# Four heads per group, masked queries, and part of the exponentials on VectorE, in an attention block with a gated MLP on one core

## The chip, the cores and the metric

One core of a Trainium2 chip runs the whole program. The metric is the time of one execution on the device in microseconds (us), as a median over runs. The kernel before takes 1070.86 us (1070.6 to 1070.98, 3 runs). All executions quoted here are recorded as fast; none was recorded as slow. TensorE is PE in the profile, its weight loads PEld, VectorE is DVE, ScalarE is ACT, GpSimd is POOL, and SP is the engine whose queue issues the DMA transfers.

## The reference, cut to what matters

```python
def reference(A_x, A_wqkv, A_wo, B_x, B_w1, B_w2, B_w3, B_w4):
    # S = 2048 tokens, D = 640, H = 32 heads of 20, F = 1536
    xn = layernorm(A_x)
    q, k, v = heads(xn @ wqkv)                            # 32 x 2048 x 20
    p = softmax(q @ k.T * 20 ** -0.5)                     # 32 x 2048 x 2048
    s = merge(p @ v) @ wo
    h = gelu(layernorm(xn) @ w1)                          # tanh form
    x1 = xn + shifted(h) @ w2
    g = silu(x1 + gelu(layernorm(x1) @ w3) @ w4)
    return A_x + s * g
```

The attention has 32 x 2048 x 2048 = 134 million exponentials. A tile of 128 keys x 512 queries x two heads is one ScalarE instruction of 1,024 elements on each of 128 partitions, so there are 1,024 such tiles.

## The kernel before

Both kernels are task graphs. Python code declares tasks with an engine, a duration, the regions they read and write, and a due time. A list scheduler inside the program then fixes the order of each engine's queue before anything runs, and each queue executes strictly in order. The heart of the kernel before:

```python
# queries of each head, masked to the head's rows, on GpSimd
T("pool", c_pool(512), lambda e, ...: e.tensor_scalar(QTP[:, qb, i, :], QT[:, st, q0:q0 + 512],
                                     self.maskh[:, j:j + 1], 0.0, op0=ALU.mult, op1=ALU.add), ...)
for kt in range(NT):                          # 16 key tiles
    for a in range(2):                        # two pairs of heads
        for jj in range(2):
            def fn(e, ...):                   # scores: four column tiles, K = 128
                for c in range(4):
                    ins = e.matmul(pb[32 * c:32 * c + 32, 0:512], KT[:, st, kt * 128 + 32 * c: kt * 128 + 32 * c + 32],
                                   QTP[:, qb, i, :], start=True, stop=True, tile_position=(0, 32 * c))
        T("act", c_act(1024), lambda e, ...: e.activation(PT[:, slot, :], self.psum[:, 1024 * sb:1024 * sb + 1024], AF.Exp,
                                                          scale=cfg.scale), ...)
    # then the product with V of the four heads: four column tiles, M = 22
...
def gelu_chain(...):                          # gelu from ScalarE's tanh: x*x, *, * on VectorE, tanh, a last multiply
    T("act", c_act(512), lambda e: e.activation(thb, wb, AF.Tanh, scale=math.sqrt(2.0 / math.pi)), ...)
```

Of the kernel before, what the change touches and what calls it, by code (L numbers as in the profile page):

```python
# [12 lines left out]
class _Heap:  # L13
# [58 lines left out]
"""Static task-graph planner for raw-BASS kernels.  # L72

Usage:
    pl = Planner()
    buf = pl.sbuf("name", nbytes)            # arena allocation (with free())
    pl.task(engine, dur_ns, emit_fn, reads=[atoms], writes=[atoms], due=...)
    pl.finish(nc, ...)                        # schedule + emit inside nc.Block

Atoms are hashable keys naming disjoint memory regions.  Dependencies  # L80
(RAW / WAR / WAW) are derived from the canonical order in which tasks are
declared.  A list scheduler then picks a per-engine order; every engine
stream is emitted with semaphore waits derived from vector clocks.
"""
# [6 lines left out]
class Task:  # L91
# [3 lines left out]
                 "acq", "rel", "stream", "sidx", "cls", "nbytes")  # L95

    def __init__(self, tid, eng, dur, fn, reads, writes, due, name, lat, is_dma):
# [24 lines left out]
        self.nbytes = 0  # L122


class Planner:
    def __init__(self):
        self.tasks = []
        self.last_writer = {}
        self.readers = defaultdict(list)
        self.pe_psum_atoms = set()  # L130
        self.arena_size = None
        self.free_list = []
        self.bufs = {}
        self.ghost = []
        self.atom_owner = {}
        self.buf_atoms = defaultdict(set)
        self.buf_range = {}
        self.buf_inherit = {}
        self.pools = {}
        self.count_instr = False  # L140
        self.dma_bw = 280.0
        self.dma_lat0 = 1900.0
        self.strict_engines = ("pe",)
        self.cls_penalty = 1e9
        self.streams = {}

# [53 lines left out]
    def task(self, eng, dur, fn, reads=(), writes=(), due=None, name="", lat=0.0,  # L200
             is_dma=False, acq=None, rel=None, stream=None, after=(), cls=0, nbytes=0):
# [3 lines left out]
        t.nbytes = nbytes  # L205
        if is_dma and nbytes:
            t.lat = self.dma_lat0 + nbytes / self.dma_bw
        t.acq = acq
# [6 lines left out]
        if stream is not None:  # L215
# [3 lines left out]
            t.sidx = len(lst) + 1  # L219
# [43 lines left out]
    def schedule(self, verbose=False):  # L263
# [13 lines left out]
        for t in reversed(tasks):  # L277
# [8 lines left out]
            t.prio = d  # L286
        for t in tasks:
            if t.cls and t.eng in self.strict_engines:
                t.prio = t.prio + self.cls_penalty
# [11 lines left out]
        done = 0  # L301
        WINDOW = 48
        while done < n:
            best = None
            for e in ENGINES:
# [7 lines left out]
                k = 0  # L313
                while h and k < WINDOW:
# [5 lines left out]
                    if t.acq is not None:  # L320
                        ps = pstate[t.acq[0]]
                        ft = min(x[0] for x in ps)
                        if ft > rt:
                            rt = ft
                    if rt <= tf + 1e-9:
                        cand = (tf, item)
                        break
# [10 lines left out]
            if st == INF:  # L338
                _log("[plan] DEADLOCK: all candidates blocked on pools")
                for e2 in ENGINES:  # L340
                    for it in ready[e2][:5]:
                        t2 = tasks[it[1]]
                        _log("   ready", e2, t2.name, "acq", t2.acq is not None)
                unsched = [t2 for t2 in tasks if t2.start is None]
                _log("   unscheduled:", len(unsched), [t2.name for t2 in unsched[:10]])
                for t2 in tasks:
                    if t2.start is not None and t2.acq is not None and id(t2.acq[1]) in held:
                        rel = [t3 for t3 in tasks if t3.rel is t2.acq[1]]
                        _log("   held by tile of", t2.name, "release task", [ (r.name, r.start, [tasks[p].name for p in r.preds if tasks[p].start is None]) for r in rel])
# [5 lines left out]
            if t.acq is not None:  # L355
                pname, handle = t.acq
                ps = pstate[pname]
                si = min(range(len(ps)), key=lambda i: ps[i][0])
                ft, rel_tid = ps[si]
                handle.slot = si  # L360
                held[id(handle)] = (pname, si)
                ps[si] = (INF, None)
                if rel_tid is not None:
                    t.preds.add(rel_tid)
                    tasks[rel_tid].succs.append((t.id, True))
            t.start = st
            t.finish = st + t.dur
            if t.is_dma and t.nbytes:
# [7 lines left out]
            if t.rel is not None:  # L376
                pname, si = held.pop(id(t.rel))
# [20 lines left out]
    def plan_sync(self, sems, dma_sems):  # L398
# [28 lines left out]
        for tid in glob:  # L427
# [3 lines left out]
            for p in sorted(t.preds, key=lambda i: (-tasks[i].finish, -tasks[i].pos)):  # L431
# [6 lines left out]
                elif pt.is_dma:  # L438
                    key = ("dma", p)
                    need = 16  # L440
# [19 lines left out]
            elif t.is_dma:  # L460
                snap[("dma", tid)] = 16
# [6 lines left out]
    def emit(self, nc, block, sems):  # L468
# [20 lines left out]
        def run_engine(ename, eng):  # L489
            cnt = _Cnt(eng) if self.count_instr else None  # L490
            for tid in self.order[ename]:
# [9 lines left out]
                if t.is_dma:  # L501
                    if t.dma_sem is not None:
                        assert ins is not None, t.name
                        ins.then_inc(t.dma_sem, 16)
# [24 lines left out]

"""Kernel generator (development version).  Uses dev.planner.Planner."""  # L530

# [3 lines left out]
I32 = mybir.dt.int32  # L535
# [13 lines left out]
class Cfg:  # L549
    def __init__(self, S=2048, D=640, H=32, F=1536, dbg=()):  # L550
# [7 lines left out]
        self.HPS = 6  # L558
        self.RPH = 21
        self.NST = (H + self.HPS - 1) // self.HPS  # L560
        self.NQUAD = H // 4
        self.TG = min(4, self.NT)
        self.NG = self.NT // self.TG
        self.scale = self.DH ** -0.5
        self.OFFSET = 60.0
        self.dbg = set(dbg)
        self.T0 = 25000.0
        self.STEP = 1000.0
        self.NSTEP = self.NQC * self.NQUAD * self.NT * 2
        self.TEND = self.T0 + self.NSTEP * self.STEP  # L570
        self.B_START = 0.25
        self.B_END = 0.8


def c_dve(n, kind="psum"):
    if kind == "psum" or kind == "1x":
        return 65 + 1.042 * n
    if kind == "2x":
        return 65 + 0.521 * n
    if kind == "4x":  # L580
        return 65 + 0.2605 * n
    if kind == "recip":
        return 65 + 6.25 * n
# [3 lines left out]
def c_act(n):  # L587
    return 70 + 0.8333 * n


def c_pe(ninstr, N):
    return ninstr * max(29.0, 0.105 * N)
# [6 lines left out]
class Gen:  # L599
# [24 lines left out]
    def free(self, name):  # L624
        self.pl.free(name)
        self.views.pop(name, None)
# [24 lines left out]

    def build(self, plan_only=False):
        nc, cfg, pl = self.nc, self.cfg, self.pl
        with contextlib.ExitStack() as es:
            ARENA = 212000
            self.arena = es.enter_context(nc.sbuf_tensor("arena", [128, ARENA], U8))
            self.psum = es.enter_context(nc.psum_tensor("psum", [128, 4096], FP32))
            pl.init_arena(ARENA)
            self.W0 = 5
            pl.pool("W", 3)  # L660
            self.program()
# [7 lines left out]
            _log(f"[gen] tasks={len(pl.tasks)} waits={pl.n_waits} dma_sems={pl.n_dma_sems} est={ms/1e3:.1f}us")  # L669
            with nc.Block() as block:  # L670
                pl.emit(nc, block, sems)

    def program(self):
        cfg = self.cfg
        self.setup_consts()
        self.alloc_persistent()
        self.load_inputs()
        self.ln1_and_transpose()
        self.load_weights_attn()
        self.alloc_attn()  # L680
        self.v_proj()
        for st in range(cfg.NST):
            self.stack_prep(st, evac_eng="act" if st == 0 else "dve")
        for nm in self.ln1_defer:
            self.free(nm)
        self.free("xnT")
        self.free("Wv")
        self.free("xbar")
        self.free("xbar_bf")
        self.out_atoms = []  # L690
        self.cur_cls = 1
        self.b_branch()
        self.cur_cls = 0
        self.attention()
        self.debug_dump()

    def setup_consts(self):
        cfg = self.cfg
        T, A = self.T, self.A
        ident = self.alloc("ident", [128], BF16)  # L700
        ones = self.alloc("ones_bf", [128], BF16)
        self.ident = ident
# [4 lines left out]
        HPS, DH = cfg.HPS, cfg.DH  # L707
        AUG0 = HPS * DH
        onesf = self.alloc("ones_f", [8], FP32)
        T("pool", 200, lambda e: e.memset(onesf[:, :], 1.0), writes=[A("ones_f")], name="onesf")  # L710
        E6 = self.alloc("E6", [8], FP32)
# [865 lines left out]
```

## Time and profile before

| kernel before | value | where it is read |
|---|---|---|
| time | 1070.86 us | median of 3 runs |
| first exponential starts | 47.1 us | timeline of ScalarE |
| stage: first exponential to the end of the last | 1013.9 us | timeline of ScalarE |
| tail after the last exponential | 11.0 us | timeline of ScalarE |
| wait of the exponentials themselves | 17.7 us | costliest groups |
| busy: ScalarE, TensorE, VectorE | 96%, 87%, 51% | busy shares |

Start, stage and tail add up, but for rounding, to the span of the profiled execution, 1071.9 us. A stage is a count of exponentials multiplied by a price, plus what ScalarE does besides, plus what it waits. The prediction shows the profile lines for these figures.

### The profile page before, as it was taken

The numbers are of one execution on the slowest core, as the hardware profiler recorded it, in microseconds if no ns is written. First come the engines' busy times: TensorE is split into PE (matmuls) and PEld (weight loads), VectorE is DVE, ScalarE is ACT, GpSimd is POOL, SyncE is SP. The second block draws the span as 40 slices with busy tenths as digits, with TensorE's granted clock in tenths as the row PEclk, the third lists the DMA queues.
The fourth block names the chain that finished last, engine by engine and source line by source line (L and its number), as shares of the span: only waits on it lengthen the run. The fifth ranks groups of instructions, "written<-read, shape, count | busy, mean of one in ns | idle before, by whom it ended". The sixth has DMA issues, their size and how long they took to land.

```text
span 1071.9 us, 38329 instructions
## 1 busy us (share of the span) xinstructions
PE 937.1 (87%) x17672; PEld 395.9 (37%) x17672; DVE 547.6 (51%) x1272; ACT 1024.4 (96%) x1175; POOL 126.2 (12%) x198
## 2 busy tenths in 40 slices
PE   3899999998978899998999899889999987777786
PEld 2454454432423344443454244224443441111132
DVE  8767766792236577378647557433457310000024
ACT  7588999999989999999999999999999999999995
POOL 4202111121001110111110111110111100011100
PEclk9999999999999999999999999999999999999998
DMA  6000000020001010031111101110011000000000
GB/s 178 16 7 14 14 3 14 7 57 2 3 14 26 22 26 21 2 100 46 27 39 46 32 21 51 33 26 15 15 27 46 27 2 2 1 2 2 1 8 32
DMA packets 62968, 27.52 MB, mean 26 GB/s; under 512 B 53208, under 2 KB 62808, under 8 KB 62808
## 3 DMA queue, kind: packets, MB, share of 16 engines
q1 hardware_dynamic: 62808, 25.08, 9.1%
q8 instruction: 138, 2.26, 0.9%
q14 instruction: 22, 0.18, 0.1%
HBM read 22.45 MB, written 2.62 MB: 23 GB/s over the span
## 4 chain that ended last, share of the span: by engine, by line
ACT 63%; PE 25%; DVE 10%; issue 1%; DMA 0%; SPq 0%; DVEq 0%
ACT arena L1190 59%; PE psum L1184 11%; PE psum L1042 4%; ACT arena L1307 3%; PE psum L1198 3%; PE psum L1407 2%; PE psum L977 1%; DVE arena L1390 1%; PE psum L1470 1%; PE psum L1364 1%; DVE arena L1131 1%; ACT arena L1483 1%; DVE arena L1092 1%; PE psum L1081 1%; DVE arena L1075 1%; DVE arena L802 1%
## 5 line engine op out<-in xcount | busy, mean ns | idle before, releaser
L1190 ACT ACTIVATE arena<-psum 128x1024 bf16<-128x1024 f32 x1024 | 961.4, 1058 | 17.7 <-PE psum L1184 15.8
L1184 PE MATMUL psum<-arena 128*32 128x512 bf16 x8192 | 626.7, 382 | 83.0 <-ACT arena L1190 66.1
L1184 PEld LDWEIGHTS psum<-arena 128*32 128x32 bf16 x8192 | 157.9, 95 | 376.4 <-ACT arena L1190 327.1
L1198 PE MATMUL psum<-arena 128*22 128x512 bf16 x2048 | 199.1, 379 | 0.9 <-ACT arena L1190 0.9
L1167 POOL TENSOR_SCALAR arena<-arena 128x512 bf16<-128x512 bf16 x128 | 95.9, 763 | 677.4 <-PE psum L1184 674.2
L1206 DVE STREAM_TRANSPOSE arena<-psum 128x512 f32<-128x512 f32 x32 | 22.8, 712 | 193.9 <-PE psum L1198 193.8
L1301 DVE CAST arena<-psum 128x512 bf16<-128x512 f32 x68 | 46.8, 688 | 85.8 <-PE psum L1450 47.3
L1450 PE MATMUL psum<-arena 128*32 128x512 bf16 x960 | 79.7, 380 | 7.6 <-DVE arena L1459 7.4
L1042 PE MATMUL psum<-arena 128*32 128x512 bf16 x960 | 74.8, 385 | 2.2 <-ACT arena L895 1.0
L1470 PE MATMUL psum<-arena 128*32 128x320 bf16 x1536 | 74.6, 299 | 1.5 <-DVE arena L1459 1.5
L1198 PEld LDWEIGHTS psum<-arena 128*22 128x22 bf16 x2048 | 52.6, 93 | 57.7 <-ACT arena L1190 1.7
L1470 PEld LDWEIGHTS psum<-arena 128*32 128x32 bf16 x1536 | 40.7, 97 | 32.9 <-DVE arena L1459 3.0
L1459 DVE SCALAR_TENSOR_TENSOR arena<-arena 128x512 bf16<-128x512 bf16 x48 | 33.1, 689 | 28.2 <-ACT arena L1307 27.9
L881 PE MATMUL psum<-arena 128*32 128x128 bf16 x960 | 28.5, 242 | 19.6 <-DVE arena L823 17.8
L1307 ACT ACTIVATE arena<-arena 128x512 bf16<-128x512 bf16 x68 | 45.1, 664 | 0.0
L1236 PE MATMUL psum<-arena 128*32 128x320 bf16 x896 | 44.6, 299 | 0.1
L1364 PE MATMUL psum<-arena 128*32 128x512 bf16 x400 | 34.4, 388 | 9.6 <-DVE arena L1390 8.8
L1450 PEld LDWEIGHTS psum<-arena 128*32 128x32 bf16 x960 | 25.4, 97 | 41.7 <-DVE arena L1459 18.4
L1480 DVE SCALAR_TENSOR_TENSOR arena<-psum,arena 128x320 bf16<-128x320 f32 x32 | 14.7, 486 | 48.2 <-PE psum L1470 45.7
L1246 DVE CAST arena<-psum 128x320 bf16<-128x320 f32 x32 | 14.7, 487 | 44.7 <-PE psum L1236 44.5
L1042 PEld LDWEIGHTS psum<-arena 128*32 128x32 bf16 x960 | 24.9, 98 | 30.0 <-DVE arena L1131 1.9
L881 PEld LDWEIGHTS psum<-arena 128*32 128x32 bf16 x960 | 20.5, 107 | 36.0 <-DVE arena L823 18.8
(104 smaller groups left out, 718.2 us busy)
## 6 DMA issues: line engine op xcount, KB each, us to landing
arena<-in_B_w_dram SPq DMA_DIRECT2D x68, 160.0 KB, 2.5
arena<-in_A_x_dram SPq DMA_DIRECT2D x8, 320.0 KB, 5.9
arena<-in_A_x_dram SPq DMA_DIRECT2D x16, 160.0 KB, 2.2
out_dram<-arena SPq DMA_DIRECT2D x16, 160.0 KB, 1.8
arena<-in_B_w_dram SPq DMA_DIRECT2D x1, 1920.0 KB, 9.3
arena<-in_A_wqkv_dram SPq DMA_DIRECT2D x10, 150.0 KB, 2.8
arena<-in_A_wqkv_dram SPq DMA_DIRECT2D x1, 800.0 KB, 9.7
arena<-in_A_wo_dram SPq DMA_DIRECT2D x4, 200.0 KB
```

What stands on the lines that cost most here:

```text
L881: ins = e.transpose(pb[32 * c:32 * c + 32, 128 * bi:128 * bi + 128], src_of(n)[:, kc * 128 + 32 * c: kc * 128 + 32 * c + 32], ident[:, :], ...
L1042: ins = e.matmul(pb[32 * c:32 * c + 32, 0:512], Wst[:, qk, kc, 32 * c:32 * c + 32], xnT[:, kc, c0:c1], start=(kc == 0), stop=(kc == KC - 1 ...
L1167: lambda e, qb=qb, i=i, st=st, j=j, q0=q0: e.tensor_scalar(QTP[:, qb, i, :], QT[:, st, q0:q0 + 512], self.maskh[:, j:j + 1], 0.0, op0=ALU. ...
L1184: ins = e.matmul(pb[32 * c:32 * c + 32, 0:512], KT[:, st, kt * 128 + 32 * c: kt * 128 + 32 * c + 32], QTP[:, qb, i, :], start=True, stop=T ...
L1190: lambda e, sb=sb, slot=slot: e.activation(PT[:, slot, :], self.psum[:, 1024 * sb:1024 * sb + 1024], AF.Exp, scale=cfg.scale),
L1198: ins = e.matmul(pb[32 * i:32 * i + 22, 0:512], VA[:, kt, h, 0:22], PT[:, slots[i // 2], 512 * (i % 2):512 * (i % 2) + 512], start=(kt == ...
L1236: ins = e.matmul(pb[32 * c:32 * c + 32, 0:HALF], OT[:, quad, 128 * nl + 32 * c:128 * nl + 32 * c + 32], Wo[:, quad, hh * HALF:(hh + 1) * H ...
L1301: T("dve", c_dve(512, "psum"), lambda e, h=h: e.tensor_copy(xb, self.wbank(h)[:, 0:512]), reads=[wa], writes=[an(0)], name=f"{tag}_x", rel=h)
L1307: T("act", c_act(512), lambda e: e.activation(thb, wb, AF.Tanh, scale=math.sqrt(2.0 / math.pi)), reads=[an(1)], writes=[an(2)], name=f"{ta ...
L1364: ins = e.matmul(pb[32 * c:32 * c + 32, 0:512], W1s[:, ws, kc, 32 * c:32 * c + 32], y2T[i][:, kc, :], start=(kc == 0), stop=(kc == KC - 1) ...
L1450: ins = e.matmul(pb[32 * c:32 * c + 32, 0:512], W3s[:, ws, kc, 32 * c:32 * c + 32], y3T[i][:, kc, :], start=(kc == 0), stop=(kc == KC - 1) ...
L1470: ins = e.matmul(pb[32 * c:32 * c + 32, 0:HALF], GTb[:, fc, 128 * nl + 32 * c:128 * nl + 32 * c + 32], W4[:, fc, hh * HALF:(hh + 1) * HALF ...
```

## The change

The intent is to take 180 of the 1,024 exponential tiles from ScalarE to VectorE, where an exponential is made by integer arithmetic on the bits of a bf16 number, and to change whatever is needed to pay for it. The diff is long. Its core, with cuts:

```diff
-        for qc in range(NQC):
-            for quad in range(NQUAD):          # queries outside, head groups inside
+        for quad in range(cfg.NQUAD):          # four heads outside
+            ...                                # projections of six heads stacked, written to DRAM, fetched per four heads
+        for qc in range(NQC):
+            if col:                            # masked queries: four diagonal blocks by DMA instead of a GpSimd multiply
+                T("sp", 4 * C_SP, lambda e, ...: [e.dma_start(self.QM[32 * i:32 * i + 32, gb, i, :],
+                                  QT[32 * i:32 * i + 32, b, 512 * qc:512 * qc + 512]) for i in range(4)], ...)
+    # number of key-tile pairs whose exponentials are shared, for each group of four heads x 512 queries
+        self.ND = ([1, 2, 3, 3], [3, 3, 3, 3], ... , [3, 3, 2, 1])
+    def score(self, e, out, b, qc, kt, i):     # a row tile: 32 partitions of keys, K = 32
+        return e.matmul(out, self.KT[32 * i:32 * i + 32, b, 128 * kt:128 * kt + 128],
+                        self.QT[32 * i:32 * i + 32, b, 512 * qc:512 * qc + 512],
+                        start=True, stop=True, tile_position=(32 * i, 0))
+    def score_both(...):                       # one pack scores 4 heads: two go to ScalarE's exp, two to VectorE
+        (h0, w0), (h1, w1) = self.wtile(), self.wtile()      # two of the three PSUM work banks
+        ...
+        T("dve", c_dve(1024), lambda e: e.tensor_scalar(U[...], psum[...], a_exp, EXP_BIAS, op0=ALU.mult, op1=ALU.add), ...)
+    def block_bits(...):                       # the exponential as a weighted sum of four bit patterns
+        for v in range(4):
+            T("dve", c_dve(w, "4x"), lambda e, ...: e.tensor_scalar(SS[:, v, 0:w], U[:, 0:w], 0.5, EXP_B[v],
+                                                                    op0=ALU.mult, op1=ALU.add), ...)
+            ...                                # each copy multiplied with V by TensorE: four products per key-tile pair
-            T("act", c_act(512), ... AF.Tanh ...)            # 68 small tanh, and the VectorE chain around them
+        T("act", 2600 + c_act(2 * KC * 512), lambda e: e.activation(hx[...], hx[...], AF.Gelu_apprx_tanh), ...)   # 4 large gelus
+        # normalisation: sums through DRAM, reciprocals, back broadcast (four small transfers), one multiply on VectorE
+        # query and key bounds in a bank that is open anyway; zeroing of QM, KT, QT by GpSimd at the start
+        # scheduler: tile modes of TensorE cost 100 ns, VectorE's queue gets strict classes, lead times are constants
```

## The prediction

> **What bounds the kernel now.** I read the busy shares first, then the chain that ended last, then the costliest groups, then the stretches, then single rows. Share and chain of the page of the kernel before:
>
> ```profile
> PE 937.1 (87%) x17672; PEld 395.9 (37%) x17672; DVE 547.6 (51%) x1272; ACT 1024.4 (96%) x1175; POOL 126.2 (12%) x198
> ...
> ACT 63%; PE 25%; DVE 10%; issue 1%; DMA 0%; SPq 0%; DVEq 0%
> ```
>
> ACT is nearly full and carries most of the chain. The groups say with what (count | busy us, mean ns | idle before it):
>
> ```profile
> L1190 ACT ACTIVATE arena<-psum 128x1024 bf16<-128x1024 f32 x1024 | 961.4, 1058 | 17.7 <-PE psum L1184 15.8
> L1184 PE MATMUL psum<-arena 128*32 128x512 bf16 x8192 | 626.7, 382 | 83.0 <-ACT arena L1190 66.1
> L1198 PE MATMUL psum<-arena 128*22 128x512 bf16 x2048 | 199.1, 379 | 0.9 <-ACT arena L1190 0.9
> L1301 DVE CAST arena<-psum 128x512 bf16<-128x512 f32 x68 | 46.8, 688 | 85.8 <-PE psum L1450 47.3
> L1307 ACT ACTIVATE arena<-arena 128x512 bf16<-128x512 bf16 x68 | 45.1, 664 | 0.0
> ```
>
> 1,024 exponentials (each two heads x 512 queries for 128 keys) waited only 17.7 us in all. Their mean of 1,058 ns is not the price, as neighbours overlap. The chain in order of time has an undisturbed run:
>
> ```profile
> 874.48 156.74 ACT arena L1190 x171
> ```
>
> 156.74/171 = 0.917 us each. In the timeline of ACT the first exponential starts at 47.10 and the last, at 1059.94, takes 1.02. So: start 47.1, a stage of 1013.9, a tail of 10.9. The stage holds 1024 x 0.917 = 939 of exponentials, 68 gelu tanh at 0.52 (a tanh at 478.76, its successor at 479.28) = 35, 16 silu tanh at 0.62 = 10: 984 of work, so 30 us (3%) lost.
>
> PE is the close second, and its 87% misleads in both directions, since matmuls overlap. Its price is read from runs of one kind in its timeline, in a dense place:
>
> ```profile
> 127.08 0.60 PE L1042 MATMUL psum<-arena 128*32 128x512 bf16 x8
> ...
> 128.18 0.39 PE L1042 MATMUL psum<-arena 128*32 128x512 bf16 x4
> ...
> 128.88 0.82 PE L1042 MATMUL psum<-arena 128*32 128x512 bf16 x12
> ```
>
> A pack of four column tiles costs 0.215 us more per pack (0.39, 0.60, 0.82). For 320 columns the same subtraction gives 0.137 (x4 0.31, x16 0.72), for 128 about 0.055. Counted from the program: 3,188 packs of 512, 960 of 320, 240 of 128 = 685 + 131 + 13 = 829 us, 77% of the span. The granted clock was 1.00 in every stretch but the end (0.79 in the last 22 us).
>
> ```profile
> 100.00:200.00 100.00, 98.38 (x1904) 44.70 (x1900) 68.52 (x178) 99.27 (x107) 13.64 (x24) 1.00 0.05 10
> ...
> 900.00:1000.00 100.00, 78.86 (x1092) 18.75 (x1088) 7.13 (x12) 100.00 (x111) 9.56 (x14) 1.00 0.01 1
> ```
>
> (PE, PEld, DVE, ACT, POOL, clock.) Late, ACT alone binds; early, PE and ACT are full together.
>
> **What the Trainium skill says.** "ScalarE: Activation LUTs", What ACT_TABLE_LOAD costs: a switch of table set is about 1,283 ns of load plus some 1,380 of drain, and every function costs 0.833 ns per element; the one load in this trace took 1.28 us, and 0.917 for 1,024 elements is 0.853 plus 0.064. "VectorE: DVE Perf Modes", The perf-mode tier table: tensor_scalar on 16-bit SBUF data runs at 4x (693 ns for 2,048 elements), on fp32 from PSUM at 1x; the trace agrees in size (PSUM cast of 512: 688 ns; SBUF tensor_scalar of 512: 309). "TensorEngine Tiling (Array Packing)", Key Properties: changing the tiling mode drains TensorE; this kernel never changes mode, so no row shows the cost. "TensorE: Matmul & The Clock Gate", Measured speedup vs the span model: four row tiles of K=32, N=512 gave 3.07x, not 4x; nothing here shows that either.
>
> **The change, part by part.** Counts are from the instruction order of the two programs.
>
> *ACT.* 844 exponentials remain; 180 tiles (17.6%) go to DVE. 844 x 0.917 = 774, against 939. The tanh form of gelu becomes a direct gelu on whole buffers: two of 5,120 and two of 12,288 elements, 0.833 per ns-element plus about 0.2 each = 4.5 and 10.4, together 30, with eight table loads x 1.28 = 10 (up to 21 with drains). Silu: 8 x 1,280 elements, 1.13 each = 9. Stage sum 823, against 984: minus 161.
>
> *PE.* An exponential fed by masked queries still needs two packs of full height, as before: 5,088 matmuls in all. A shared tile scores four heads in one pack of row tiles (776 matmuls). But each moved block of two key tiles needs four weighted products more: 1,440 matmuls. Total 2,857 packs of 512, 896 of 320, 160 of 128 = 614 + 123 + 9 = 746 us, minus 83. To this add the row packs' shortfall (194 packs x 0.215 x (4/3.07 - 1) = 13) and the mode switches: 12 in a typical stretch of 26 exponentials. I estimate 0.17 us each, the part of a pack's 0.39 that is not hidden when nothing follows (0.39 - 0.215): 2 us per stretch, some 60 in all.
>
> *DVE.* Added: 180 PSUM tiles of 1,024 to integers. Three casts of 320 took 1.29 in a row, 0.40 each; so 1,024 is about 1.13, 180 x 1.13 = 204. 120 tensor_scalars of 2,048 and 120 of 4,096: 0.69 and 1.23 if 4x holds, 230. Removed: three ops of the gelu chain (29.7 + 21.0 + 31.0 = 82) and its last multiply (58), the norm bounds of keys and queries (about 90 net), part of normalising (20). 548 - 250 + 434 = about 730 us, over 80% of the new span: full, not the bound.
>
> *DMA.* Stacked projections, masked queries and reciprocal sums pass through DRAM, 553 issues against about 130. They are small and planned ahead; GB/s was 26 on average, so bandwidth is no issue; each hop costs about 2 us (2.2 for 160 KB before), off the path if the plan holds.
>
> *Start and end.* Before, the first exponential waited for sums in the transposes' evictions (0.78 instead of 0.58 on ACT), three PSUM banks, and a long bound of norms. Now four banks, plain copies, a short maximum: I take off 12 us, giving 35; GpSimd's bigger memsets ahead of the rstd power give some back. Tail: final products of 0.6, four normalising ops 2.4, 1 for matmuls, 4.7 for evictions and adds, 2 for the store = 11, as before.
>
> *Sum.* Floor: 35 + 823 + 11 = 869. It isn't reached, as PE is now as full as ACT. Per stretch of 26 exponentials ACT needs 23.84, and PE, counted in queue order, 20.6 to 22 in most and 25 to 29 in those with a big gelu, plus 2.4 for switches and row packs. Taking the larger of both in each stretch, with gelu time added to ACT where it stands, gives 850 for the stage instead of 823. 35 + 850 + 11 = 896. I add nothing for jitter, because PE work can also slide between stretches: 897.
>
> **The rivals.** (a) *ACT stays the bound, and the plan hides PE:* 869 to 880. For it: before, ACT lost 3% with PE at 98% busy. Against: PE's slack per exponential falls, and it gets mode switches. (b) *PE becomes the bound:* switches of 0.3 to 0.4 and row packs that don't overlap add 2 to 3 us per stretch, in about 32 stretches: 940 to 960. For it: nothing measured speaks for a cheap switch. Against: two kinds of matmul are rare within a stretch. (c) *DVE's in-order queue:* a 1.2-us operation stands in front of an eviction, PE waits for a bank and ACT for PE; 0.5 us per block x 90 = 45, to 940. If the integer operations ran at 2x, DVE would gain 190 us of work, be over-full, and the time would pass 950. (d) *DMA latency:* the masked queries arrive late at a group's start, 31 x 1 to 2 us: 930 to 960. The two-deep buffer speaks against it.
>
> **Range and chances.** Low: floor plus 3 = 872. High: one of (b) to (d) at half size, 932. Even two of the three at full size (897 + 63 + 63) stay under 1,049, 2% below the time before, so faster 0.97, same 0.02, slower 0.01.
>
> **What would show it.** ACT: 844 exponentials at 0.917 in undisturbed runs; first one at 35; four gelus at 4.5 and 10.4. PE: idle before the scores, ended by ACT, shrinks far below 83 us; the exponentials' own idle time (17.7) grows to some 30, ended by PE. DVE: 4,096 elements in about 1.3 us. Wrong if: the exponentials wait over 60 us, or mostly for DVE or a DMA behind PE; a row pack costs over 0.3; the first one starts after 40.

## The result, and the profile after

The changed kernel takes 914.5 us (912.82 to 915.75, 4 runs), beside 1070.92 us for the kernel before in the same rounds. The ratio is 0.8534 (95% interval 0.8518 to 0.8551). Ratios here are the mean time of one kernel's fast runs over that of the other's of the same rounds, so they are not quite the ratio of the medians. The prediction was 897 (872 to 932): it is 17.5 us too low, and the result lies in the range.

The page of the kernel after, busy shares and chain that ended last:

```profile
PE 838.0 (92%) x15654; PEld 367.2 (40%) x15654; DVE 714.5 (78%) x999; ACT 863.2 (95%) x911; POOL 37.8 (4%) x69
...
ACT 56%; PE 34%; DVE 6%; DMA 3%; issue 1%; SPq 0%; ACTq 0%
```

ScalarE lost 161 us of busy time and TensorE 99, while VectorE gained 167. TensorE has a larger part of the chain (34% against 25%). The costliest groups of the kernel after (count | busy us, mean ns | idle before, what ended most of it):

```profile
L1369 ACT ACTIVATE arena<-psum 128x1024 bf16<-128x1024 f32 x844 | 789.5, 1034 | 25.4 <-PE psum L1327 16.1
L1345 PE MATMUL psum<-arena 128*32 128x512 bf16 x5088 | 388.7, 382 | 19.3 <-ACT arena L1369 15.1
...
L1401 DVE TENSOR_SCALAR arena<-psum 128x1024 uint16<-128x1024 f32 x177 | 216.1, 1221 | 83.3 <-PE psum L1327 82.0
L1308 DVE TENSOR_SCALAR arena<-arena 128x2048 uint16<-128x2048 uint16 (+1 forms) x240 | 219.2, 956 | 2.2 <-PE psum L1319 1.7
...
L1327 PE MATMUL psum<-arena 32*128 32x512 bf16 x776 | 82.0, 387 | 14.1 <-DVE arena L1401 5.7
```

The first line is the answer to the 17.7 us of before. The exponentials now wait 25.4 us, mostly for L1327, the row tiles that score four heads at once. The second line and the last answer to TensorE's 83.0 us before the scores: 19.3 us are left before the scores from masked queries and 14.1 before the row tiles, 33.4 together, so most of the slack that TensorE had behind ScalarE is gone. The third and fourth lines are the new work of VectorE. By form, the 4,096-element operations take 1,225 ns and those of 2,048 take 687.

The timeline of ScalarE has the start and the price of a gelu (start us, length us, what):

```profile
39.54 21.45 ACT L1369 ACTIVATE arena<-psum 128x1024 bf16<-128x1024 f32 x23 [0.48 <-PE psum L1327]
...
176.71 1.28 ACT L1670 ACT_TABLE_LOAD   x1
178.01 4.47 ACT L1670 ACTIVATE arena<-arena 128x5120 bf16<-128x5120 bf16 x1
182.50 1.28 ACT L1369 ACT_TABLE_LOAD   x1
```

The first exponential starts at 39.5 and the last ends at 902.5: a stage of 863.0 and a tail of 10.6. ScalarE's work in it is 844 x 0.917 = 774, plus two gelus of 4.47 and two of 10.45 = 30, plus eight table loads of 1.283 = 10, plus eight silus of 1.272 = 10: 824. The stage loses 863 - 824 = 39 us. Of these, 25.4 are the idle time in the first group line. The other 14 are found in 176 intervals of 0.96 to 1.1 us between starts of neighbouring exponentials, where 0.92 is undisturbed. They are waits of 40 to 180 ns, too short to appear as idle time because neighbours overlap.

Two stretches of the kernel after (PE, PEld, DVE, ACT, POOL, clock, DMA share, GB/s):

```profile
100.00:200.00 100.00, 93.71 (x1624) 37.64 (x1626) 86.85 (x105) 99.90 (x103) 0.68 (x2) 1.00 0.20 55
...
700.00:800.00 100.00, 91.15 (x1784) 43.39 (x1776) 69.45 (x85) 94.37 (x96) 2.60 (x2) 0.97 0.21 58
```

Early, ScalarE is full even where VectorE and TensorE are busier than later. The loss lies later: ScalarE drops to 94% while TensorE is at 91%. So the load of an engine over 100 us does not tell where ScalarE waits. The second largest single wait of an exponential is 3.48 us, at 581.9. The chain in order of time, followed back from it:

```profile
577.53 1.49 DVE arena L1742
579.02 0.41 DVE arena L1734
...
579.48 1.81 PE psum L747 x48
581.29 0.22 PE psum L1319 x4
581.51 0.36 PE psum L1327 x4
...
581.89 1.02 ACT arena L1369
```

L1742 is the last operation of a silu on VectorE. L1734 stands behind it in VectorE's queue and frees a PSUM work bank. The projection packs L747 wait for the bank, and the row tile for the next exponential stands behind them in TensorE's queue. TensorE stands still for only 0.65 of the 3.48 us, in front of L747. For the rest it works, on products with V and projections that stand ahead of the scores. The same holds in general: added up over the trace, TensorE is at work in 21.0 of the 24.9 us that the exponentials after the first one wait. What makes ScalarE wait is thus mostly what TensorE does first. Whether less work or another order would help cannot be read from it, and the experiments ask that.

### The profile page after: what moved, and what is told of

The parts are those of the page before. It is cut to its first block, busy times and chain, and to the rows that moved or that the text cites. A ratio compares the mean times of both kernels' runs of the same rounds, so it can differ in the third digit from the quotient of the medians.

```text
span 913.2 us, 34227 instructions
## 1 busy us (share of the span) xinstructions
PE 838.0 (92%) x15654; PEld 367.2 (40%) x15654; DVE 714.5 (78%) x999; ACT 863.2 (95%) x911; POOL 37.8 (4%) x69
## 4 chain that ended last, share of the span: by engine, by line
ACT 56%; PE 34%; DVE 6%; DMA 3%; issue 1%; SPq 0%; ACTq 0%
ACT arena L1369 51%; PE psum L747 13%; PE psum L1345 11%; PE psum L1286 4%; PE psum L1327 3%; PE psum L1319 2%; DMA arena<-recips 2%; DVE arena L1401 2%; ACT arena L1723 1%; ACT arena L1670 1%; DMA recips<-arena 1%; DVE arena L1308 1%; ACT arena L986 1%; DMA arena<-in_A_x_dram 1%; ACT arena L1739 1%
## 5 line engine op out<-in xcount | busy, mean ns | idle before, releaser
L1369 ACT ACTIVATE arena<-psum 128x1024 bf16<-128x1024 f32 x844 | 789.5, 1034 | 25.4 <-PE psum L1327 16.1
L1345 PE MATMUL psum<-arena 128*32 128x512 bf16 x5088 | 388.7, 382 | 19.3 <-ACT arena L1369 15.1
L747 PE MATMUL psum<-arena 128*32 128x320 bf16 (+1 forms) x5952 | 360.7, 335 | 12.3 <-DVE arena L1124 5.3
L1401 DVE TENSOR_SCALAR arena<-psum 128x1024 uint16<-128x1024 f32 x177 | 216.1, 1221 | 83.3 <-PE psum L1327 82.0
L1308 DVE TENSOR_SCALAR arena<-arena 128x2048 uint16<-128x2048 uint16 (+1 forms) x240 | 219.2, 956 | 2.2 <-PE psum L1319 1.7
L747 PEld LDWEIGHTS psum<-arena 128*32 128x32 bf16 x5952 | 153.3, 97 | 153.5 <-issue 21.6
L1286 PE MATMUL psum<-arena 128*22 128x512 bf16 x1688 | 163.7, 381 | 1.7 <-ACT arena L1369 1.4
L1319 PE MATMUL psum<-arena 128*22 128x512 bf16 x1440 | 115.0, 380 | 2.6 <-DVE arena L1308 2.5
L1327 PE MATMUL psum<-arena 32*128 32x512 bf16 x776 | 82.0, 387 | 14.1 <-DVE arena L1401 5.7
L1286 PEld LDWEIGHTS psum<-arena 128*22 128x22 bf16 x1688 | 43.1, 92 | 58.1 <-issue 13.4
L1327 PEld LDWEIGHTS psum<-arena 32*128 32x128 bf16 x776 | 20.9, 91 | 92.6 <-ACT arena L1369 59.0
L1319 PEld LDWEIGHTS psum<-arena 128*22 128x22 bf16 x1440 | 35.2, 92 | 43.1 <-DVE arena L1308 6.8
L1523 DVE SCALAR_TENSOR_TENSOR arena<-psum,arena 128x320 bf16<-128x320 f32 x32 | 15.6, 488 | 17.7 <-PE psum L747 17.2
L935 DVE BATCH_NORM_STATS2 arena<-arena 128x6 f32<-128x320 bf16 x52 | 23.8, 482 | 3.5 <-DMA arena<-in_A_x_dram 3.5
L1734 DVE TENSOR_TENSOR arena<-psum,arena 128x320 bf16<-128x320 f32 x32 | 15.6, 487 | 13.1 <-PE psum L747 12.8
L1723 ACT ACTIVATE arena<-arena 128x12288 bf16<-128x12288 bf16 x2 | 20.9, 10446 | 0.0
```

The lines of the kernel that those rows point to most:

```text
L747: ins = e.matmul(pb[32 * c:32 * c + 32, 0:N], lhsT(k, c), rhs(k, c), start=(k == 0), stop=(stop and k == nk - 1), tile_position=(0, 32 * c))
L935: lambda e, li=li, n=n, hh=hh: e.bn_stats(st[:, li, 6 * hh:6 * hh + 6], xn[:, n, hD * hh:hD * hh + hD]),
L1286: ins = e.matmul(pb[32 * i:32 * i + 22, 0:512], VA[:, ql, kts[i // 2], i, :], PT[:, slots[i // 2][0].slot, 512 * (i % 2):512 * (i % 2) + 512],
L1308: T("dve", c_dve(w, "4x"), lambda e, v=v, dst=dst: e.tensor_scalar(dst, U[:, 0:w], 0.5, EXP_B[v], op0=ALU.mult, op1=ALU.add), reads=halves ...
L1319: ins = e.matmul(pb[32 * i:32 * i + 22, 0:512], wv, dst[:, at:at + 512].bitcast(BF16), start=first, stop=final, tile_position=(0, 32 * i))
L1327: return e.matmul(out, self.KT[32 * i:32 * i + 32, b, 128 * kt:128 * kt + 128], self.QT[32 * i:32 * i + 32, b, 512 * qc:512 * qc + 512], s ...
```

## The experiments

Twelve kernels ran. All take the kernel before along as the reference of their rounds (medians 1071.58 to 1073.41). The rounds ran on different chips, so the ratios compare better than the times. "Stage" and "first" are read from ScalarE's timeline of each profile, "idle" is the exponentials' own.

| kernel | us | ratio to before | first | stage | idle | TensorE, VectorE busy us |
|---|---|---|---|---|---|---|
| before | 1070.9 | 1 | 47.1 | 1013.9 | 17.7 | 937, 548 |
| after | 914.5 | 0.8534 | 39.5 | 863.0 | 25.4 | 838, 715 |
| nd0 | 1064.9 | 0.9926 | 39.6 | 1011.8 | 11.3 | 919, 301 |
| before_drop (wrong result) | 957.1 | 0.8921 | 47.2 | 897.4 | 58.9 | 887, 549 |
| dve_light (wrong result) | 929.6 | 0.8668 | 39.5 | 877.1 | 38.9 | 844, 611 |
| pe_light (wrong result) | 908.6 | 0.8470 | 39.5 | 855.6 | 21.3 | 812, 711 |
| dve_same (wrong result) | 916.4 | 0.8545 | 42.4 | 859.8 | 22.7 | 840, 622 |
| pe_same (wrong result) | 908.5 | 0.8473 | 38.8 | 855.8 | 22.5 | 823, 713 |
| zeros_moved | 919.8 | 0.8578 | 43.8 | 864.0 | 26.1 | 843, 718 |
| on_moved | 963.1 | 0.8974 | 40.3 | 911.4 | 69.5 | 854, 714 |
| zero_half | 916.0 | 0.8541 | 40.1 | 863.8 | 25.9 | 841, 715 |
| norm_turn | 932.0 | 0.8694 | 39.7 | 878.9 | 40.2 | 842, 732 |
| row_scores | 955.1 | 0.8915 | 41.7 | 900.1 | 52.1 | 851, 714 |
| norm_replanned | 908.1 | 0.8467 | 42.7 | 853.1 | 22.0 | 844, 731 |

### nd0: the changed kernel without the exponentials on VectorE

```diff
-        self.ND = ([1, 2, 3, 3], [3, 3, 3, 3], ... , [3, 3, 2, 1])
+        self.ND = ([0, 0, 0, 0],) * 8
```

> The changed kernel with no exponential on VectorE: all 1,024 on ACT, no weighted products, no mode switches after the first group. Theory (the gain is the exponentials that left ACT): first exponential at 39.5, stage 1,024 x 0.92 = 942 plus 49 of gelu, silu and table loads plus some 15 of waits, tail 10.7: 1,050 to 1,065 us, within 2% of the kernel before. Rival (the new order, direct gelu, masked queries by DMA and stacked projections carry a good part of the gain): under 1,030.

It measured 1064.86 us (ratio 0.9926, interval 0.9903 to 0.9949). Its exponentials in the costliest groups:

```profile
L1361 ACT ACTIVATE arena<-psum 128x1024 bf16<-128x1024 f32 x1024 | 952.4, 1056 | 11.3 <-PE psum L1337 10.0
```

All the rest of the change together is worth 0.7%, some 8 us. The 180 moved tiles are worth the remaining 150 us (1064.86 - 914.5), or 0.83 each where one costs 0.917. The start of 39.6 is that of the changed kernel, so the start's gain of 7.5 us comes from the rest. The stage is only 2.1 us shorter than before.

### before_drop: the kernel before, with the same 180 exponentials left out

This gives a wrong result on purpose (relative error 0.68), since nothing is put in their place.

```diff
-                        T("act", c_act(1024), ... AF.Exp ...)
+                        if not skip:           # the key tiles and head pairs that the changed kernel moves
+                            T("act", c_act(1024), ... AF.Exp ...)
```

> The kernel before without the same 180 exponentials (wrong on purpose: the products read older probabilities; TensorE's work is unchanged, VectorE gets none of theirs). Theory A (ACT alone bounds the kernel before): 1,071 - 180 x 0.917 = 906. Theory B (TensorE is a close second, full in the stretches with projections): 920 to 940, with the exponentials' idle time well above 17.7 us. If it comes near 914, the changed kernel's extra work on VectorE and TensorE costs nothing that a free removal would not also have cost.

It measured 957.08 us (ratio 0.8921). Chain and exponentials:

```profile
PE 57%; ACT 32%; DVE 9%; issue 1%; DMA 1%; ACTq 0%; SPq 0%; DVEq 0%
...
L1194 ACT ACTIVATE arena<-psum 128x1024 bf16<-128x1024 f32 x844 | 798.0, 1034 | 58.9 <-PE psum L1185 31.9
```

Freeing ScalarE alone, even for nothing, turns the chain over to TensorE, and the exponentials wait 58.9 us. The changed kernel is 43 us faster although it also computes the moved exponentials. Some 8 of these are its earlier start. The other 35 are what the rest of the change brings once ScalarE is unloaded, after paying for the moved exponentials; in nd0 it brought 2 us in the stage. That TensorE's smaller work does it fits the waits, as TensorE is busy in all of the 58.9 us, but is not shown alone: before_drop was also planned anew, with due times that still leave 1.0 us for each of the 1,024 tiles.

### dve_light and pe_light: less work on one engine, planned anew

Both give wrong results on purpose. dve_light makes two of the four bit patterns instead of four; pe_light multiplies only two of the four with V.

```diff
-            T("dve", c_dve(w, "4x"), ... dst = SS[:, v, 0:w] ...)
+            if v < 2: T("dve", c_dve(w, "4x"), ... dst = SS[:, v % 2, 0:w] ...)      # dve_light
-            for n, (j, pairs, kts) in enumerate(blocks):
+            for n, (j, pairs, kts) in enumerate(blocks) if v % 2 == 0 else ():        # pe_light
```

> The changed kernel with only two of the four shifted copies made on VectorE, each read twice (wrong on purpose); TensorE multiplies as before. VectorE loses about 110 of its 714 us. Theory 1 (the exponentials wait because VectorE's in-order queue hands PSUM banks back late): 12 to 20 us faster than 914.5, so 894 to 902, and idle time before the exponentials well under 25 us. Theory 2 (TensorE's own capacity): 0 to 5 us faster.

> The changed kernel with all four copies made on VectorE but only two of them multiplied (wrong on purpose): 720 matmuls, 180 packs x 0.215 = 39 us less on TensorE. Theory 2 (TensorE's capacity): 15 to 25 us faster, 890 to 900. Theory 1 (VectorE's queue): 0 to 6 us faster.

dve_light measured 929.56 (0.8668), slower than the changed kernel with 104 us less on VectorE. pe_light measured 908.63 (0.847). A kernel that only loses work cannot lose 15 us by it unless the order changed, and it had: the scheduler runs again on every edit. These two runs are confounded. Their lesson is that a new order alone moves the time by more than the effect looked for.

### dve_same and pe_same: less work in the same order

The repair was to let the scheduler plan with the full durations and then emit smaller instructions, so that every queue keeps its order. Both results are wrong on purpose.

```diff
-            ... e.tensor_scalar(dst, U[:, 0:w], 0.5, EXP_B[v], ...)
+            cut = 16 if v > 1 else w                                                  # dve_same
+            ... e.tensor_scalar(dst[:, 0:cut], U[:, 0:cut], 0.5, EXP_B[v], ...)
-                        ins = e.matmul(pb[32 * i:32 * i + 22, 0:512], wv, dst[:, at:at + 512].bitcast(BF16), ...)
+                        N = 512 if v % 2 else 16                                      # pe_same: first and third cut
+                        ins = e.matmul(pb[32 * i:32 * i + 22, 0:N], wv, dst[:, at:at + N].bitcast(BF16), ...)
```

> As dve_light, but every engine keeps the changed kernel's exact order of instructions; the third and fourth shifted copies are only cut to 16 columns each (wrong on purpose). dve_light had been replanned, which confounds it. VectorE loses about 100 us. Theory 1 (waits come from VectorE's in-order queue): 12 to 20 us faster, 894 to 902. Theory 2 (TensorE's capacity): 0 to 5 us faster.

> As pe_light, but in the changed kernel's exact order; the first and third of the four weighted products are cut to 16 columns (wrong on purpose): 180 packs x (0.215 - some 0.03) = 33 us less on TensorE. Theory 2: 15 to 25 us faster. Theory 1: 0 to 6 us faster, as pe_light was (5.9).

dve_same: 916.38 (914.54 to 917.64). Its busy shares, then its exponentials:

```profile
PE 839.8 (92%) x15654; PEld 368.5 (40%) x15654; DVE 622.1 (68%) x999; ACT 862.7 (95%) x911; POOL 39.8 (4%) x70
...
L1373 ACT ACTIVATE arena<-psum 128x1024 bf16<-128x1024 f32 x844 | 789.0, 1035 | 22.7 <-PE psum L1331 13.9
```

VectorE has 92 us less to do and the time is the same. The stage is 3.2 us shorter, and the first exponential comes 2.8 us later, which I put down to one more memset that this kernel needs at the start. So 92 us of VectorE's load are worth 3 us in the stage: it is not the bound.

pe_same: 908.5 (907.22 to 909.63). The same lines of its page:

```profile
PE 822.5 (91%) x15654; PEld 354.6 (39%) x15654; DVE 713.3 (79%) x999; ACT 858.9 (95%) x911; POOL 38.1 (4%) x69
...
L1370 ACT ACTIVATE arena<-psum 128x1024 bf16<-128x1024 f32 x844 | 785.2, 1040 | 22.5 <-PE psum L1328 14.0
```

TensorE's busy time fell by 15.5 us (I had counted on twice that) and the time by 6 us. The interval of its ratio, 0.846 to 0.8485, lies below that of the changed kernel. So TensorE's load counts a little, at about 0.4 us for each us. The exponentials' own idle time fell by 2.9 us, and their short waits (the intervals of 0.96 to 1.1 us) by 3.8. The large waits stayed where they were: 4.0 us at 76.6, 3.5 at 577, 2.1 at 740, against 4.1 at 77.4, 3.5 at 581.9, 2.1 at 746.6 in the changed kernel. They do not go with this much of TensorE's load, in this order.

### zeros_moved and zero_half: the memsets at the start

The changed kernel zeroes three buffers on GpSimd before the powers of the first rstd, which start at 11.93 us instead of 7.41 before. zeros_moved puts the memsets behind those powers and keeps every other queue's order. zero_half leaves them where they are and writes 32-bit words, half as many elements.

```diff
+            for name in ("qt0", "kt0", "qm0"):                                        # zeros_moved
+                pl.move(name, pl.named["ln1_4_pow"].id)
-        ... e.memset(self.QM[:, :, :, :], 0.0) ...
+        ... e.memset(self.QM[:, :, :, :].bitcast(FP32), 0.0) ...                      # zero_half, and KT, QT alike
```

> The changed kernel with GpSimd's three large memsets (3.5 + 1.8 + 1.8 us) moved behind the first half's rstd powers; all other queues keep their order. The first power started at 11.93 when the memsets ended, its input was ready at about 9.8: the first exponential should come about 2 us earlier than 39.5 and the kernel take 912 to 913. If the V projection that stands ahead of the second half's transposes is what sets the start, nothing changes.

> Correct; the changed kernel's order on every queue, but the three memsets of zeros on GpSimd at the start write 32-bit words instead of 16-bit ones, so half as many elements (3.5 and two times 1.8 us before). Theory: these memsets cost the start twice, once because the powers of the first rstd stand behind them on GpSimd and once because they hold off VectorE's 4x operations (with the memsets moved later, two of those took 4.07 us), so halving them brings the first exponential from 39.5 to 37 to 38.5 and the time to 911 to 913. Rival: the start is set by the V projections that stand in TensorE's queue from 18.5 us on, fed by DMA, and nothing comes of it (39.5, 914.5).

zeros_moved: 919.82 (0.8578), slower by 5, with the first exponential at 43.8. Its stage is the same (864.0), so the start is all of it. The timelines of VectorE and then of GpSimd in zeros_moved:

```profile
12.12 4.07 DVE L983 TENSOR_SCALAR arena<-arena 128x640 bf16<-128x640 bf16 x2
```

```profile
12.32 3.68 POOL L915 MEMSET arena<- 128x4096 bf16 x1
```

Two VectorE operations that take 0.79 together elsewhere took 4.07, and the second ended at 16.19, just after the memset's end at 16.00. This is the shared port that the Trainium skill describes: "SBUF — State Buffer", Who interferes with whom, says that a VectorE instruction in a two-port mode and a GpSimd instruction exclude each other for a whole instruction, and whichever starts first holds the pair. The trace agrees.

zero_half: 915.96 (0.8541), no change. Its memsets were done at 8.55 and the powers started at 9.80, 2.1 us earlier than in the changed kernel. The timelines of VectorE and then of GpSimd in zero_half show where that went:

```profile
13.40 2.88 DVE L949 TENSOR_SCALAR arena<-arena 128x640 bf16<-128x640 bf16 x2
```

```profile
13.49 1.25 POOL L1224 MEMSET arena<- 128x256 bf16 x1
14.80 1.30 POOL L1225 MEMSET arena<- 128x256 bf16 x1
```

GpSimd, free earlier, went on to the next two memsets of its queue, and these landed on the same kind of VectorE operation. Then TensorE took its 33 packs of V projections, and the second half of the transposes stood behind them. The timelines of TensorE in the changed kernel and then in zero_half:

```profile
18.55 6.83 PE L747 MATMUL psum<-arena 128*32 128x320 bf16 x132 [0.53 <-DVE arena L1044]
```

```profile
18.31 7.60 PE L747 MATMUL psum<-arena 128*32 128x320 bf16 x132 [0.53 <-DVE arena L1044]
```

In zero_half they start 0.24 us earlier and end 0.53 us later, and the first exponential is 0.54 us later too. The same 33 packs take longer because of the clock: packs start 0.267 us apart until about 20.9 us in the changed kernel and 22.2 us in zero_half, and 0.136 apart from then on. The granted clock is recorded as full from 20.88 and 22.22 us. So zero_half's small gain was lost to a clock that turned full 1.3 us later, one execution against one. Both theories of the start are therefore too simple: the memsets do cost VectorE time, but most of one such cost removed before 14 us was spent again on the next memsets. That the V projections set the start is read from the traces and was not tried by itself.

### on_moved: the normalising multiply later in VectorE's queue

VectorE waited up to 2.2 us for the reciprocals that come back through DRAM. The edit moves the multiply that needs them up to eight places back in VectorE's queue and leaves all other orders alone.

```diff
+            for quad in range(7):
+                for qc in range(4):            # up to 8 places later, never past the next group's eviction
+                    pl.move(f"on{quad}_{qc}", ...)
```

> The changed kernel with the normalising multiply of each group (which waits for the broadcast reciprocals) moved up to 8 places back in VectorE's queue; nothing else moves. It stood there idle for 9.6 us in all. If that hold-up reaches ACT: 5 to 9 us faster, 905 to 910. Rival: the store of the heads behind it on the DMA queue waits longer, later masked queries come late, and the time stays or rises.

It measured 963.06 (0.8974), 49 us slower. Two groups of its page:

```profile
L1414 ACT ACTIVATE arena<-psum 128x1024 bf16<-128x1024 f32 x844 | 792.7, 1033 | 69.5 <-PE psum L1372 36.8
...
L777 PE MATMUL psum<-arena 128*32 128x320 bf16 (+1 forms) x5952 | 367.3, 340 | 40.1 <-DMA arena<-in_B_w_dram 21.8
```

TensorE now waits 21.8 us for weights from DRAM. In the waits of the DMA queue, the transfer that stores the finished heads stands 255.4 us waiting for the moved multiply, against 74.8 in the changed kernel. All transfers share one queue in order, so weights and masked queries stand behind it. Rival (d) of the prediction, DMA latency, did not happen in the changed kernel (its waits show TensorE held up 0.2 us by DMA in all), but this shows how near it is.

### norm_turn: normalisation without DRAM

The last quad normalises with two transposes on VectorE. This edit does that for all quads and so takes 112 small transfers out of the DMA queue.

```diff
-        if last:
+        if True:                               # transpose, reciprocal, multiply, transpose back on VectorE
             ...
-        ZT, RB = self.ZT, self.RB              # sums to DRAM, reciprocals back, multiply
```

> Correct; normalisation of all quads as the last one does it already: VectorE transposes in 32x32 blocks, a reciprocal, a multiply and a transpose back, instead of four small transfers through DRAM for each group. The order is planned anew. VectorE gets some 38 us more work, the DMA queue loses 112 small transfers. Theory (order and the single DMA queue keep the stage above ScalarE's floor, not VectorE's load): exponentials' own idle falls from 25 to 15 to 22 us, time 900 to 912. Rival (VectorE is nearly full, as dve_same should have shown but did not): idle over 35 us, time 922 to 940. As a new plan alone can shift 10 us either way, a change under 10 us says little about the load.

It measured 932.01 (0.8694), 17.5 us slower, with the exponentials' own idle at 40.2. That is within what the rival said. But it had been planned anew, VectorE's busy time rose by only 17 us, and dve_same had shown that 92 us on VectorE are worth 3 us. So the cause was still open.

### row_scores: no masked queries

```diff
-            col = self.grp > 0
+            col = False
```

> Correct; no masked queries: the scores of all groups as row tiles of 32 partitions with four heads at once, as the first group does it, with the order planned anew. If a switch of tile mode is 105 ns each way as measured, an exponential's two quarter packs cost about what the masked product costs and TensorE's busy time stays within 20 us of 838: time 905 to 930. Rival (masked queries are needed because row tiles at 32 partitions or the switches cost more): TensorE becomes the bound, exponentials' idle over 60 us, time over 950.

It measured 955.07 (0.8915), 41 us slower than the changed kernel, and the reason is neither theory's. TensorE's busy time is 851 us, as the first theory said (though at a lower clock), and a switch of tile mode costs the same 105 ns, at some 1,480 switches instead of 414. But the granted clock fell to 0.931 on average, 0.929 to 0.931 in all four runs, where the changed kernel has 0.988 to 0.993. The stretch from 800 to 900 us of row_scores:

```profile
800.00:900.00 100.00, 91.45 (x922) 24.72 (x918) 66.89 (x86) 86.00 (x90) 0.72 (x2) 0.71 0.19 60
```

The same product with V there, in the timeline of TensorE of row_scores, first in a slowed and then in an undisturbed place:

```profile
839.63 0.61 PE L1286 MATMUL psum<-arena 128*22 128x512 bf16 x4
...
844.91 0.40 PE L1286 MATMUL psum<-arena 128*22 128x512 bf16 x4
```

A pack takes 0.61 us where 0.40 is usual. The clock record has only full and half clock: half for 23.9 us from 820.5 and again from 847.8 us, so the mean of 0.71 is a mixture. The clock explains only part of the 41 us: up to 600 us it is 0.97 or more, and there ScalarE is already up to 14 us less busy in a stretch of 100 us than in the changed kernel (81.8 against 95.9 from 500 to 600), under a plan that is also new. The split between clock and plan stays open. What lowers the clock stays open too. That three quarters of every masked query are zeros does not explain it alone: nd0, with masked queries from the second group on, also fell to 0.974 to 0.976, with half clock for 44 us of its stage, where the changed kernel has 10 us. There the half clock met a TensorE with time to spare (busy 31% to 76% in the longer stretches); in row_scores it met a busy one.

### norm_replanned: the operations of norm_turn in another order

The scheduler got the fixed costs that the traces show, and its lead times were searched anew on its own forecast. The halved memsets of zero_half, which had moved nothing, are in it too.

```diff
-        self.mode_cost = 100.0
+        self.mode_cost = 105.0
-        self.T0 = 38000.0;  self.STEP = 960.0
+        self.T0 = 42264.725;  self.STEP = 876.145
-        self.EARLY, self.WO, self.B1, self.B2 = 15570.0, 20580.0, (0.64, 0.7), (3.06, 0.95)
+        self.EARLY, self.WO, self.B1, self.B2 = -58652.577, -40424.444, (0.568, 0.615), (3.155, 0.658)
-        self.LEAD, self.LEAD0, self.VLEAD = 65220.0, 56120.0, 9440.0
+        self.LEAD, self.LEAD0, self.VLEAD = 52304.806, 25930.17, 20923.231
-    c_dve: 185 + ... ;  c_act: 90 + ...
+    c_dve: 156 + ... ;  c_act: 66 + ...
```

> Correct; the same operations as norm_turn (normalisation on VectorE, no transfers through DRAM for it) with the halved zeroing of zero_half, which moved nothing; only the order is another: the planner was given the fixed costs that the traces show (VectorE 156 ns and ScalarE 66 ns beside the work, 105 ns for a switch of tile mode), and its nine lead times were searched anew on its own forecast, which says 905 us where it said 942 for norm_turn (measured 932) and 921 for the changed kernel (measured 914.5). Theory (norm_turn lost its 17 us to the order and not to VectorE's 17 us more of work): 900 to 918 us, exponentials' own idle 15 to 28 us. If it is under 912 it beats both kernels. Rival (the work moved to VectorE costs it): 925 to 940, idle about 40 as in norm_turn.

It measured 908.08 us (906.26 to 908.8, 5 runs; ratio 0.8467, interval 0.8455 to 0.8478), with a correct result. Its busy shares, then its exponentials:

```profile
PE 844.2 (93%) x15654; PEld 350.7 (39%) x15654; DVE 730.5 (81%) x1027; ACT 856.4 (94%) x911; POOL 33.7 (4%) x69
...
L1369 ACT ACTIVATE arena<-psum 128x1024 bf16<-128x1024 f32 x844 | 783.1, 1049 | 22.0 <-PE psum L1327 13.2
```

All engines have the work that they had in norm_turn, yet the time is 24 us shorter and the idle time went from 40.2 to 22.0. The loss of norm_turn was thus its order, and what goes with it: half clock for 17 us of norm_turn's stage and 3 us here. The kernel is also 6 us faster than the changed kernel and beats both, with a stage of 853.1 instead of 863.0 although its first exponential comes 3.2 us later. In its trace, 707 of 843 intervals between exponentials are under 0.96 us, against 628 in the changed kernel. What of the 6 us the missing transfers give and what the new order gives was not separated, because the changed kernel's own operations did not run under a renewed search.

## Why the prediction was right or wrong

**The direction and the floor were right.** The prediction put ScalarE's work in the stage at 823 us, and it measures 824. The exponential's price (0.917 to 0.920), the gelus (4.47 and 10.45 against 4.5 and 10.4), the loads and the tail (10.6 against 11) hold. nd0 shows that the moved exponentials carry 150 us of the gain.

**The start failed as a size.** "I take off 12 us, giving 35" measured 7.5 us off, giving 39.5. This is 4.5 of the 17.5 us. "GpSimd's bigger memsets ahead of the rstd power give some back" is right in that the power started 4.5 us later than before, but zero_half shows that taking the cost away does not give it back. What the step left out, as the trace shows it, is the 6.83 us of V projections that stand before the second half's transposes in TensorE's queue, about 10 of their 33 packs before the clock was full.

**The step from floor to stage had the right size of answer for a partly wrong reason.** The prediction added 27 us "as PE is now as full as ACT", from larger-of-both counts per stretch. The stage lost 39. That is the other 13 us, rounded (850 against 863). What is shown to be wrong is that TensorE's capacity alone sets the loss: norm_turn and norm_replanned have the same work and stages 25.8 us apart. Its load has a part in it: pe_same took 15.5 us off TensorE's busy time and got 6 back, with the large waits in place. A count of work per stretch, the larger of both engines, cannot see waits for a PSUM bank and for the place in a queue. How the 39 us divide between load and order stays open.

**Two terms of TensorE's sum were too large.** The mode switch was estimated at 0.17 us. In the trace a row pack follows the start of the pack before it after 0.320 us, where column packs follow each other after 0.215: 0.105 per switch. The trace has 414 switches, so that is 43 us, not 60. The shortfall of the row packs was put at 13 us from the skill's 3.07 times, but the four row tiles start within 13 ns of each other and the pack takes no longer than a column pack (387 ns a matmul against 382), so next to nothing of it is seen. These two errors made TensorE look some 30 us fuller than it is, and hid that the count by capacity alone gives too little loss.

**DVE "full, not the bound" is shown.** Predicted at about 730 us, it is 714.5, with the 4,096-element operation at 1.225 us (predicted 1.23), and dve_same shows that its load does not set the time. Rival (c), the in-order queue of VectorE, exists as one of the links in the chain at 577 to 582, not as 45 us.

**The rivals.** (a), 869 to 880, was too good: it needs a plan that hides everything, and norm_replanned with a stage of 853.1 is still 29 us above the floor. (b), 940 to 960, needed switches of 0.3 to 0.4. (d) did not happen, though on_moved reached 963 by disturbing the DMA queue. Of the stated signs, "the first one starts after 40" missed being true by half a microsecond; the idle time of "some 30, ended by PE" measured 25.4, ended by PE; TensorE's idle before the scores, far below 83, is 33.4. "A row pack costs over 0.3" is true if the switch is counted with it (0.320) and false without it.

**Slips that changed nothing.** 35 + 850 + 11 is 896, not 897. Half of the largest rival, 63 us, would put the high end at 928, not 932. In the kernel before, the clock was below 1.00 in one earlier stretch too (0.98 from 300 to 400 us). And "ACT lost 3% with PE at 98% busy" joins two places: in the stretch with TensorE at 98% ScalarE was at 99.27%, and it lost most elsewhere.

## What to carry to other kernels

When two engines are nearly full, relieve the second in the same change that moves work off the first. Here before_drop and nd0, one half each, bring 10.8% and 0.7%, where both together bring 14.7% and also do the moved work. In this kernel, with three engines above 75%, a new order of the queues moved the time by 24 us, more than taking 92 us off VectorE or 15 off TensorE did, so compare experiments only with the order held fixed, and give a static scheduler the durations that the trace shows. A freed engine starts its next task earlier: ask what that task then collides with, as the memsets did here.

## What the Trainium skill lacked or had wrong

- "TensorEngine Tiling (Array Packing)", Key Properties: it says that a change of tiling mode drains TensorE and gives no figure. Here the switch between column packs of K=128 and row packs of K=32 costs 105 ns each way (0.320 us from start to start instead of 0.215).
- "TensorE: Matmul & The Clock Gate", Measured speedup vs the span model: it gives 3.07 times for four row tiles of K=32, N=512. In these streams the four start within 13 ns of each other and the pack costs what a column pack costs, beside the switch. No single-tile time was measured here for a speedup of the same definition.
- The same page does not say how long half clock can last in a TensorE that hardly pauses. In row_scores the granted clock was half for 23.9 us twice (from 820.5 and 847.8 us), with TensorE busy 93% and 96% of them and no pause over 0.53 us from 813.7 us to their end. Matmuls of 0.61 us instead of 0.40 confirm the record. What set it is not shown.
- "ScalarE: Activation LUTs", What ACT_TABLE_LOAD costs: the load of 1,283 ns agrees, but the drain of some 1,380 ns is not seen. Between the start of the load at 176.71 and the start of the gelu at 178.01 lie 1.30 us, and the load starts as the exponential before it ends.
